# Retention and two MLPs on one core: whole weight rows summed in SBUF, and two changes to when loads are requested

## The chip, the cores and the metric

One core of a Trainium2 chip runs the whole program in one launch. The metric is the device time of one execution in microseconds (us); before is given as the median of three runs, and lower is better. The traces come from the hardware profiler, one execution each.

## The reference

Batch 4, 768 positions, 8 heads of 64, so 3072 tokens of width 512, all in float32. Retention comes first, then a squared-relu MLP (512 to 2048 to 512), then an RMS-normed gated MLP (512 to 1536 to 512):

```python
for t in range(S):
    state = gamma[None, :, None, None] * state + np.einsum('bhd,bhe->bhde', k[:, :, t], v[:, :, t])
    y[:, :, t] = scale * np.einsum('bhd,bhde->bhe', q[:, :, t], state)

h = np.maximum(x @ w_in, 0.0)            # first MLP
x = h * h @ w_out

rms = np.sqrt(np.mean(x * x, axis=-1, keepdims=True) + 1e-06)
xn = x / rms * rms_g                     # second MLP
g = xn @ w_gate
silu = g * (1.0 / (1.0 + np.exp(-g)))
val = xn @ w_val
return (silu * val @ w_out)
```

The weights arrive as 64-bit floats; the kernel turns them into 32-bit ones itself.

## The kernel before

**Products.** Each float32 operand is kept as a high and a low part (`split`: ScalarE casts the high part, VectorE subtracts for the low part), and every product is three matmuls, high by high, high by low, low by high (`mm3`, lines 259 to 261; `proj`, line 301). From the second half of the first MLP on, blocks of 2x2 tiles are multiplied in seven products instead of eight, named P1 to P7. That needs sums and differences of weight tiles ("units"), made once and stored in DRAM: `ui` and `uo` for the first MLP's in- and out-weights, `wu` for the second MLP's gate and value weights, `uo2` for its out-weights. A ring of seven buffers streams them back.

**Stages.** (1) Retention of the first four chunks and the first MLP's block 0 (`block1(0, ...)`, 16 iterations `f`), during which the first MLP's 32 weight tiles are loaded and converted; they stay in SBUF as `W["i", f]` and `W["o", f]`. (2) `block1(1, ...)`, again 16 iterations: per iteration one projection (12 matmuls into `ph`), and the out-products of the iteration before (`out1`, 12 matmuls into `pa` and `pb`); on every even `f` one chunk of retention is visited (`visit`: values, the state, and the next chunk's scores into both `ph` banks). (3) `in_phase` and `in_pair`, then `Out.run`, for the second pair of token blocks, then the third. (4) The second MLP, `pair` by `pair`: six pairs for a block of tokens, each with products P2, P1, P5, P6, P7, P3, P4 (12 matmuls each), then its out-products.

**Order.** The program is scheduled by hand (`tc.manual_schedule`): each engine works in program order. SyncE (SP) issues nearly all DMAs, in program order too, waiting where a buffer or datum isn't ready. `later` collects stores that are issued at the next call of `stores()`. Most tiles come from one pool of 38 slots (`slot`, 128 partitions x 1024 floats). 32 of them are the first MLP's weights in stage 2.

**Making units.** `made_units` takes two tiles `rows` (four weight tiles, whole rows) and makes a sum and differences in five steps, each ended by `yield`: a sum and a difference; the unit P5; P7; P6; P3. P1, P2 and P4 are stored straight from the weights (`keep_units`, `keep_out`, `keep_in`). `whole_rows` fills `rows` for group `q`: for groups 0 and 1 (`2 * q < NCL`) as high + low of the tiles in SBUF, four VectorE sums in two steps; for groups 2 and 3 by two loads from `kept`, to which `finish1` had stored the converted weights in stage 1 (a step of its own, line 1243). In stage 2 `made` (out-weights, groups 0 to 3) is advanced once per even and three times per odd iteration, `made_in` (in-weights, groups 2, 3, 0, 1) once per iteration from `f` = 4 on, and the rest in stage 3.

`tick` converts one weight tile per call (a ScalarE operation, two VectorE ones, and for the second MLP's out-weights a split). After `more_steps(W2_SOON)` at `f == MORE_AT` (line 1330) 25 tiles of the second MLP follow, one per iteration, in stage 2's last iterations, stage 3, and the first steps of `Out.run` (`extra1`).

In stage 4's first block of tokens, `pair` also makes the units of gate and value weights (`make_unit`, quarters `q` reloaded from `wq`), and `made_late` (line 173) those of the out-weights: `first`, `second` and `third` are called after P1, after P6 and after P3 of each pair, and advance it once, twice and once. `first` of pair 0 then runs two steps of the last norm (`background`): a `fold` of squares on VectorE and a request for column sums, which TensorE does in `second` (`sums`, line 337), right behind P6.

**Chunks.** After a visit of chunk `c`, `after_visit` requests chunk `c + 2`: `load` (v and k in natural order, line 892 or 894), then `load_q` (line 902), then `load_k` (line 907). GpSimd scales v (`decay_v`, line 935) and q (`decay_q`, line 924) in later iterations.

Of the kernel before, what the change touches and what calls it, by code (L numbers as in the profile page):

```python
# [38 lines left out]
COMING = (0, 1, 2, 5, 8, 9, 13, 16, 17, 18, 19, 20)  # L39
AHEAD = 5  # L40
EARLY = 24
MORE_AT = 9
W2_SOON = 25
X_AT = (11, 12, 17, 18, 23, 24)

# [13 lines left out]
def retention_then_two_mlps(  # L59
# [16 lines left out]
    uo2 = [[dram.tile([128, 2, 512], F32, name=f"up{q}{k}") for k in range(7)] for q in range(NQ2)]  # L76
    wu = [[dram.tile([128, 2, 512], F32, name=f"wu{n}{k}") for k in range(7)] for n in range(NPR)]
    rows2 = [[dram.tile([128, 2, 512], F32, name=f"rows_p{q}{r}") for r in range(2)] for q in range(NQ2)]
    kept = {(k, n): dram.tile([128, 2, 512], F32, name=f"rows_{k}{n}") for k in "io" for n in range(NCL, 2 * NQ)}

    ones = const.tile([128, D], F32, name="ones")
    g_sb = const.tile([128, KC], F32, name="g_sb")
# [4 lines left out]
    def slot(name, dt=F32):  # L87
        return wp.tile([128, 2, 512], dt, tag="w", name=name)
# [39 lines left out]
    def finish1(key, f, eng=None):  # L128
        t = slot(f"w_{key[0]}{key[1]}", F32R)
        W[key] = t  # L130
        nc.scalar.copy(t[:, 0, :], f)  # L131
        if key[1] >= 2 * NCL:
            nc.sync.dma_start(kept[key[0], key[1] // 2][:, key[1] % 2, :], f)
        return lambda: low(eng or nc.vector, t[:, 1, :], f, t[:, 0, :])

    row_tiles = {}
# [34 lines left out]
        yield  # L171

    def made_late():
        for q in range(NQ2):
            rows = [slot("rows") for _ in range(2)]
            for to, kept_rows in zip(rows, rows2[q]):
                nc.sync.dma_start(to, kept_rows)
            yield
            yield from made_units(uo2, q, rows, lambda: slot("sm")[:, 0, :])

    def finish2(key, f):
        k, n = key
# [26 lines left out]
    def magnitude(i):  # L209
        if i < upto[0] and i not in sizes:  # L210
            key = steps[i][1]
            if key[0] == "p":
                sizes[i] = row_of(key[1])
            elif key[0] in "io" and key[1] >= 2 * NCL and i % 3 == 0:
                sizes[i] = tp.tile([128, TB], F32, tag="y", name="f")
            else:
                sizes[i] = cf.tile([128, 512], F32, tag="f", name="f")
            nc.scalar.activation(sizes[i], loads[i].bitcast(F32)[:, :, 1], AF.Prelu, scale=REBIAS, alpha=NEGATIVE)
# [646 lines left out]
    with tc.manual_schedule():  # L865
# [17 lines left out]
        def load(c):  # L883
            if c < NCH:
                both[c] = rp.tile([128, 2, 512], F32, tag="vk", name="vkt")
                chunk[c] = [None, None] + [both[c][:, i].rearrange("p (a h d) -> p a h d", a=NP, h=2) for i in range(2)]
                if c > CB:
                    load_v(c)

        def load_v(c):  # L890
            if c // B == CPB - 1:
                nc.sync.dma_start(both[c][:, 0], vk[c][:, 0])
            else:
                nc.sync.dma_start(both[c], vk[c])
# [142 lines left out]
        def after_visit(c, x, kv):  # L1037
            x.put(columns_of(c), halves())
            take_state(c, kv)
            load(c + 2)  # L1040
            load_q(c + 2)
            load_k(c + 2)

        decays = slot("decays")
        given, factors = (xp.tile([6 * NP, C + 2 * 512 + H], dt, tag="x", name="factors") for dt in (F32, F32R))
# [112 lines left out]
        def first_states(f):  # L1158

            if f == 2:  # L1160
                take_state(0, into_state(0))
            if f == 0:
                decay_q(CB, nc.vector)
            if f == 1:
                load(CB + 1)
                load_q(CB + 1)
                decay_v(CB, nc.gpsimd)
                decay_v(1, nc.gpsimd)
            for c, n in ((1, 2), (2, 5), (3, 9)):
                if f == n - 1:  # L1170
                    load_kn(c)
                if f == n and c > 1:
                    decay_v(c, nc.vector)
            if f == 2:
                decay_q(CB + 1, nc.vector)
            if f == 3:
                nc.sync.dma_start(g_sb, rmsg)
# [60 lines left out]

        def whole_rows(key, q):
            rows = row_tiles[key, q] = [slot("rows") for _ in range(2)]  # L1240
            if 2 * q >= NCL:
                for r in range(2):
                    nc.sync.dma_start(rows[r], kept[key, 2 * q + r])
                yield
                return
            for r in range(2):
                for c in range(2):
                    w = W[(key, 4 * q + 2 * r + c)].bitcast(F32)
                    plus(rows[r][:, c, :], w[:, 0, :], w[:, 1, :])
                yield  # L1250
# [74 lines left out]
        def last1(f):  # L1325
            stores()
            if f >= RING_AT:
                more_ring()
            next(made, None)
            if f == MORE_AT:  # L1330
                more_steps(W2_SOON)
            if f > MORE_AT:
                tick()
            if f >= 4:
                next(made_in, None)
            if f in (10, 12, 14):
                next(coming_xs)
# [95 lines left out]
        coming_x = raw_x(xs2, X)  # L1433

        def extra1(n, y):
            if n < 3:
                stores()
                tick()
            if n == NOUT - 8:
# [142 lines left out]
        for s in range(NS):  # L1582
# [5 lines left out]
            for p in range(NPR):  # L1588
# [8 lines left out]
                        next(making, None)  # L1597

                def first():
                    make_late(1)  # L1600
                    if p == 0:
                        background()
                        background()
# [4 lines left out]

                def second():
                    nonlocal coming  # L1610
                    make_late(2)
                    if p == 0 and due:
                        sums(pb[1])
                    background()
# [122 lines left out]
```

## Time and profile before

| | |
|---|---|
| median of three runs | 1104.53 us (1103.72 to 1105.84) |
| the profiled execution | 1104.13 us |
| its span, first to last instruction | 1102.4 us |
| TensorE busy | 1083.9 us, 98% of the span |
| VectorE / ScalarE / GpSimd busy | 793.6 / 573.5 / 77.1 us |
| mean granted clock of TensorE | 0.994 |
| DMA | 299.82 MB, 272 GB/s over the span |

Idle time of VectorE or ScalarE counts only where TensorE ends up waiting for it. A trace row gives the start and the duration in us, engine, line, operation, out<-in by the names of the tiles, shape, and count; in brackets stands the idle time of that engine before it and what ended it. Matmuls are pipelined, so the time between two starts says more than a duration: 12 matmuls of 512 columns take about 2.72 us from start to start.

### The profile page before, as it was taken

How to read it: one execution, taken by the hardware profiler on the slowest of the kernel's cores; microseconds unless marked ns; L12 is line 12 of the kernel's file. 1: busy time of each engine (PE TensorE's matmuls, PEld its weight loads, DVE VectorE, ACT ScalarE, POOL GpSimd, SP SyncE). 2: the span in 40 equal slices, each digit the busy share in tenths (PEclk: the TensorE clock that was granted, in tenths of full speed). 3: DMA queues.
4: the chain of work that ended last, by engine and by line, in shares of the span. 5: the costliest groups of instructions: out<-in, count | busy, mean ns of one | idle time of the engine just before them, and what ended most of it. 6: DMA issues, size and time to landing. Idle time of an engine off the chain costs nothing.

```text
span 1102.4 us, 16685 instructions
## 1 busy us (share of the span) xinstructions
PE 1083.9 (98%) x6281; PEld 890.5 (81%) x6281; DVE 793.6 (72%) x1103; ACT 573.5 (52%) x880; POOL 77.1 (7%) x65
## 2 busy tenths in 40 slices
PE   9999999899999999999999989999999999999998
PEld 7888888678878888888888768788888888888887
DVE  6988687699948995678778877996333797333585
ACT  5776445567666546784456545553232554333442
POOL 3000142214320000000000000000000000000000
PEclk9999999899999999999999989999999999999999
DMA  9869699999999679976558989767667567656663
GB/s 363 310 226 324 237 318 362 365 374 352 355 407 317 214 256 382 377 269 208 201 189 309 367 302 343 251 211 252 197 210 270 193 210 249 195 194 196 196 211 116
DMA packets 108164, 299.82 MB, mean 272 GB/s; under 512 B 11012, under 2 KB 34332, under 8 KB 108084
## 3 DMA queue, kind: packets, MB, share of 16 engines
q1 hardware_dynamic: 107904, 298.51, 76.8%
q8 instruction: 50, 0.82, 0.3%
q10 hardware_dynamic: 180, 0.24, 0.1%
q14 instruction: 30, 0.25, 0.1%
HBM read 210.09 MB, written 88.62 MB: 271 GB/s over the span
## 4 chain that ended last, share of the span: by engine, by line
PE 82%; DMA 7%; DVE 6%; ACT 2%; issue 1%; SPq 1%; POOL 0%; DVEq 0%; POOLq 0%; ACTq 0%
PE ph L301 9%; PE ph L259 9%; PE ph L260 9%; PE ph L261 9%; PE pa L259 7%; PE pa L261 7%; PE pa L260 7%; PE pb L259 4%; PE pb L261 4%; PE pb L260 4%; PE pr L259 3%; PE pr L261 3%; PE pr L260 3%; DMA rows<-rows_p 1%; DMA ui<-made 1%
## 5 line engine op out<-in xcount | busy, mean ns | idle before, releaser
L482 ACT CAST o<-act 128x1024 fp32r<-128x1024 f32 x101 | 105.6, 1052 | 111.2 <-DVE act L107 53.5
L100 DVE TENSOR_TENSOR o<-act,o 128x1024 fp32r<-128x1024 f32 x101 | 122.9, 1219 | 27.9 <-ACT o L482 27.8
L260 PE MATMUL ph<-o,ring 128*128 128x512 f32 x228 | 88.6, 389 | 0.0
L259 PE MATMUL ph<-o,ring 128*128 128x512 f32 x228 | 88.5, 388 | 0.0
L261 PE MATMUL ph<-o,ring 128*128 128x512 f32 x228 | 88.5, 388 | 0.0
L259 PE MATMUL pb<-xop,ring 128*128 128x512 f32 x192 | 76.3, 397 | 5.2 <-DVE part L110 4.0
L301 PE MATMUL ph<-xh,w_i 128*128 128x512 f32 x248 | 81.1, 390 | 0.0
L259 PE MATMUL ph<-xop,ring 128*128 128x512 f32 x192 | 75.3, 392 | 1.1 <-DVE part L110 0.6
L261 PE MATMUL pb<-xop,ring 128*128 128x512 f32 x192 | 75.7, 394 | 0.0
L260 PE MATMUL pb<-xop,ring 128*128 128x512 f32 x192 | 75.7, 394 | 0.0
L259 PE MATMUL pa<-xop,ring 128*128 128x512 f32 x192 | 74.9, 390 | 0.0
L260 PE MATMUL ph<-xop,ring 128*128 128x512 f32 x192 | 74.8, 389 | 0.0
L261 PE MATMUL ph<-xop,ring 128*128 128x512 f32 x192 | 74.7, 389 | 0.0
L261 PE MATMUL pa<-xop,ring 128*128 128x512 f32 x192 | 74.7, 389 | 0.0
L260 PE MATMUL pa<-xop,ring 128*128 128x512 f32 x192 | 74.7, 389 | 0.0
L107 DVE TENSOR_TENSOR act<-act 128x1024 f32<-128x1024 f32 x60 | 73.1, 1219 | 0.3
L110 DVE TENSOR_TENSOR part<-pr,part 128x512 f32<-128x512 f32 x38 | 25.8, 689 | 54.4 <-ACT part L114 53.1
L114 ACT COPY part<-ph 128x512 f32<-128x512 f32 x52 | 30.3, 589 | 57.8 <-PE ph L261 57.8
L760 ACT ACTIVATE t<-part 128x512 f32<-128x512 f32 x54 | 34.1, 632 | 49.8 <-DVE part L110 49.8
L301 PEld LDWEIGHTS ph<-xh,w_i 128*128 128x128 f32 x248 | 46.5, 188 | 10.3 <-ACT w_o L131 0.4
L260 PEld LDWEIGHTS ph<-o,ring 128*128 128x128 f32 x228 | 42.8, 188 | 9.3 <-DVE o L100 0.4
L259 PEld LDWEIGHTS ph<-o,ring 128*128 128x128 f32 x228 | 42.8, 188 | 8.9
(255 smaller groups left out, 2632.3 us busy)
## 6 DMA issues: line engine op xcount, KB each, us to landing
ring<-wu SPq DMA_DIRECT2D x84, 512.0 KB, 4.3
ring<-up SPq DMA_DIRECT2D x63, 512.0 KB, 4.2
ring<-uo SPq DMA_DIRECT2D x56, 512.0 KB, 4.3
ring<-ui SPq DMA_DIRECT2D x42, 512.0 KB, 7.2
wu<-ring SPq DMA_DIRECT2D x42, 512.0 KB, 6.0
raw<-w1i SPq DMA_DIRECT2D x16, 512.0 KB, 7.4
raw<-w1o SPq DMA_DIRECT2D x16, 512.0 KB, 8.4
vkt<-vk SPq DMA_DIRECT2D x16, 512.0 KB, 5.1
```

Of the source, the lines that this page charges most:

```text
L100: eng.tensor_tensor(out=dst_l, in0=src, in1=dst_h.bitcast(F32), op=ALU.subtract)
L107: eng.tensor_tensor(out=out_, in0=a, in1=b, op=ALU.subtract)
L110: eng.tensor_tensor(out=out_, in0=a, in1=b, op=ALU.add)
L114: nc.scalar.copy(dst[:, m], acc[m])
L259: nc.tensor.matmul(acc, ah, bh, start=start, stop=False, **more)
L260: nc.tensor.matmul(acc, ah, bl, start=False, stop=False, **more)
L261: nc.tensor.matmul(acc, al, bh, start=False, stop=stop, **more)
L301: nc.tensor.matmul(h, w[:, a, k * 128:(k + 1) * 128], x[b][k], start=n == 0, stop=n == len(order) - 1)
L482: nc.scalar.copy(h, src)
L760: nc.scalar.activation(t, g, AF.Silu)
```

## The change

Five edits. `finish1` no longer stores converted weights to DRAM, `kept` goes, and `whole_rows` makes every group as sums of the tiles in SBUF (so its tiles `f` all come from one pool). `made_in` starts at iteration 1 instead of 4 and is advanced twice in iterations 5 to 8; `MORE_AT` goes from 9 to 12, and `extra1` does six conversions instead of three. `made_late` requests the rows of group `q + 1` in the fourth step of group `q`, and is advanced two, one and one times in pairs 0 to 2, then once each. `load_v` is called after `load_q` and `load_k` in `after_visit`.

```diff
-MORE_AT = 9
+MORE_AT = 12
...
     def finish1(key, f, eng=None):
...
-        if key[1] >= 2 * NCL:
-            nc.sync.dma_start(kept[key[0], key[1] // 2][:, key[1] % 2, :], f)
...
     def made_late():
+        def fetch(q):
+            rows = [slot("rows") for _ in range(2)]
+            for to, src in zip(rows, rows2[q]):
+                nc.sync.dma_start(to, src)
+            return rows
+
+        rows = fetch(0)
         for q in range(NQ2):
-            rows = [slot("rows") for _ in range(2)]
-            for to, kept_rows in zip(rows, rows2[q]):
-                nc.sync.dma_start(to, kept_rows)
             yield
-            yield from made_units(uo2, q, rows, lambda: slot("sm")[:, 0, :])
+            for n, _ in enumerate(made_units(uo2, q, rows, lambda: slot("sm")[:, 0, :])):
+                if n == 3 and q + 1 < NQ2:
+                    coming = fetch(q + 1)
+                yield
+            if q + 1 < NQ2:
+                rows = coming
...
-            elif key[0] in "io" and key[1] >= 2 * NCL and i % 3 == 0:
-                sizes[i] = tp.tile([128, TB], F32, tag="y", name="f")
...
-                if c > CB:
-                    load_v(c)
-
         def load_v(c):
+            if c >= NCH:
+                return
...
             load(c + 2)
             load_q(c + 2)
             load_k(c + 2)
+            load_v(c + 2)
...
                 load(CB + 1)
+                load_v(CB + 1)
                 load_q(CB + 1)
...
         def whole_rows(key, q):
             rows = row_tiles[key, q] = [slot("rows") for _ in range(2)]
-            if 2 * q >= NCL:
-                for r in range(2):
-                    nc.sync.dma_start(rows[r], kept[key, 2 * q + r])
-                yield
-                return
             for r in range(2):
                 for c in range(2):
                     w = W[(key, 4 * q + 2 * r + c)].bitcast(F32)
                     plus(rows[r][:, c, :], w[:, 0, :], w[:, 1, :])
                 yield
...
-            if f >= 4:
+            if f:
+                next(made_in, None)
+            if 4 < f < 9:
                 next(made_in, None)
...
-            if n < 3:
+            if n < 6:
                 stores()
                 tick()
...
                 def first():
-                    make_late(1)
+                    make_late(2 if p < 3 else 1)
...
                 def second():
                     nonlocal coming
-                    make_late(2)
+                    make_late(1)
```

## Rows read from the trace of the kernel before

**Rows 1.** What TensorE waited for: total us, times, longest.
```profile
PE pb L259 <- DVE part L110: 4.0, 1, 4.0
PE ph L947 <- issue: 4.7, 1, 4.7
...
PE pa L260 <- DVE s L100: 0.7, 1, 0.7
PE pa L947 <- POOL qnt L924: 0.7, 1, 0.7
PE ph L259 <- DVE part L110: 0.6, 1, 0.6
```

**Rows 2.** Stretches: length, busy us per engine, granted clock, DMA share, GB/s.
```profile
188.91:202.77 13.86, 13.86 (x129) 11.44 (x128) 6.34 (x13) 7.69 (x13) 3.40 (x3) 1.00 1.02 377
202.77:224.49 21.72, 17.02 (x130) 13.71 (x129) 18.28 (x31) 11.95 (x21) 4.09 (x3) 0.84 0.97 356
573.05:592.93 19.88, 19.88 (x101) 16.06 (x100) 14.22 (x23) 9.96 (x17) 0.00 (x0) 1.00 0.90 326
...
633.02:659.51 26.49, 22.08 (x85) 17.38 (x84) 19.31 (x33) 10.16 (x19) 0.00 (x0) 0.87 0.85 317
659.51:678.67 19.16, 19.16 (x85) 15.85 (x84) 12.67 (x21) 9.92 (x19) 0.00 (x0) 1.00 0.81 296
```

**Rows 3.** VectorE in order of time, near 200 us.
```profile
205.88 0.69 DVE L110 TENSOR_TENSOR sm<-rows 128x512 f32<-128x512 f32 x1 [7.62 <-DMA rows<-rows_o]
```

**Rows 4.** ScalarE in order of time, near 200 us.
```profile
206.61 0.62 ACT L103 CAST made<-sm 128x512 fp32r<-128x512 f32 x1 [7.25 <-DVE sm L110]
```

**Rows 5.** VectorE in order of time, near 650 us.
```profile
650.25 0.69 DVE L110 TENSOR_TENSOR sm<-rows 128x512 f32<-128x512 f32 x1 [3.37 <-DMA rows<-rows_p]
...
653.49 1.28 DVE L110 TENSOR_TENSOR part<-pb,part 128x512 f32<-128x512 f32 x2
```

**Rows 6.** Two sums of high and low parts on VectorE.
```profile
145.88 1.28 DVE L110 TENSOR_TENSOR rows<-w_o 128x512 f32<-128x512 f32 x2
```

**Rows 7.** Stretches 124 to 150, 150 to 175 and 175 to 198, together.
```profile
sum 74.00, PE 74.00 PEld 60.93 DVE 60.00 ACT 37.51 POOL 27.22; mean PE 24.67 PEld 20.31 DVE 20.00 ACT 12.50 POOL 9.07
```

**Rows 8.** The stretch of the first half of one mask.
```profile
121.96:122.93 0.97, 0.97 (x5) 0.79 (x6) 0.91 (x4) 0.12 (x1) 0.00 (x0) 1.00 0.59 220
```

**Rows 9.** VectorE and GpSimd in order of time, near 154 us.
```profile
154.40 1.67 DVE L110 TENSOR_TENSOR sm<-rows 128x512 f32<-128x512 f32 x1
...
153.78 1.73 POOL L378 TENSOR_TENSOR y<-y 128x512 f32<-128x512 f32 x1
```

**Rows 10.** The page's 40 slices, tenths: VectorE busy, TensorE's granted clock.
```profile
DVE  6988687699948995678778877996333797333585
...
PEclk9999999899999999999999989999999999999999
```

**Rows 11.** SP's issues in order of time, near 307 us.
```profile
306.60 0.33 SPq L892 DMA_DIRECT2D vkt<-vk  x1
307.83 0.39 SPq L902 DMA_DIRECT2D qnt<-qT  x1
```

**Rows 12.** SP's issues of the second MLP's rows, groups 0 and 2.
```profile
577.30 1.63 SPq L177 DMA_DIRECT2D rows<-rows_p  x2
...
641.54 1.94 SPq L177 DMA_DIRECT2D rows<-rows_p  x2
```

**Rows 13.** The chain of waits, 573 to 600 us: start, us, what.
```profile
577.80 6.82 DMA rows<-rows_p
```

**Rows 14.** VectorE in order of time, near 580 us.
```profile
579.92 1.94 DVE L110 TENSOR_TENSOR sq<-sq 128x1024 f32<-128x1024 f32 x2
...
585.99 0.69 DVE L110 TENSOR_TENSOR sm<-rows 128x512 f32<-128x512 f32 x1
```

**Rows 15.** TensorE in order of time, near 584 us.
```profile
584.02 0.64 PE L337 MATMUL pb<-sq,ones 128*32 128x128 f32 x16
```

**Rows 16.** ScalarE in order of time, near 139 us.
```profile
138.73 0.62 ACT L103 CAST made<-rows 128x512 fp32r<-128x512 f32 x1 [2.98 <-PE pb L261]
```

More of the change, by code (lines that the diff above doesn't have):

```diff
@@ L78, in retention_then_two_mlps @@
     rows2 = [[dram.tile([128, 2, 512], F32, name=f"rows_p{q}{r}") for r in range(2)] for q in range(NQ2)]
-    kept = {(k, n): dram.tile([128, 2, 512], F32, name=f"rows_{k}{n}") for k in "io" for n in range(NCL, 2 * NQ)}
     ones = const.tile([128, D], F32, name="ones")
```

## The prediction, made before the result was known

> **What bounds the kernel now.** I read the page first: TensorE is busy 98% of the span, so nothing but its few idle microseconds, and the stretches in which its clock is low, can be won. The list of what TensorE waited for [rows 1] names those idles; the five that the change can touch are shown. Two matter: 4.7 us before a chunk's scores and 4.0 us before a product of the second MLP's first block. The table by stretch [rows 2] gives their full price. From one chunk's visit to the next takes 13.86 us, but the stretch from 202.77 takes 21.72, so 7.86 are lost: 4.70 idle, and 17.02 us of TensorE work where 13.86 is normal, that is 3.16 us at the lower of its two levels (1.2 instead of 2.4 GHz; granted clock 0.84). In the first block of the second MLP a quiet pair of steps (from 659.51) takes 19.16 us; the pair from 633.02 takes 26.49, 7.33 lost, of which 22.08 - 19.16 = 2.92 at the low clock.
>
> Next, who was late. At 198 VectorE stands 7.62 us before the first sum over `rows`, until a load of whole rows of the first MLP's out-weights lands [rows 3]. ScalarE, in order, is held 7.25 us at the cast of that sum [rows 4]; the relu that would free the score bank is queued behind it, and TensorE behind that. Before 650.25 it is the same with the second MLP's out-rows: 3.37 us on the load, everything behind it is late, and so is the sum `part` for which TensorE waits [rows 5].
>
> **The change, part by part.**
> 1. *Sums in SBUF for the rows of groups 2 and 3 of both first-MLP matrices.* The load at 195 to 206 is gone, and so is what it holds. The whole 7.86 us of that stretch goes [rows 2], and with it the backlog that makes VectorE late for `s` once more at 239, 0.7 us [rows 1]. I book 7.86 + 0.73 = 8.59.
>
> What it adds: 16 sums of 128x512 (4 groups of 4), two of which take 1.28 us clean [rows 6], so 16 x 0.6 = 9.6 us of VectorE. They come before the time they are needed, since the in-rows now start in iteration 1 instead of 4 and run double-paced in iterations 5 to 8, while the second MLP's conversions start three iterations later. Counting steps iteration by iteration (a sum step 1.2, the five others 1.3, 0.6, 1.2, 1.2, 0.6 us), iterations 1 to 9 get 10.9 us more. Between 124 and 198 VectorE is busy 60.0 of 74 us [rows 7], so 14.0 us are free. It fits, but 3 us from full, and the order within an iteration matters: the first half of a mask, 0.97 us [rows 8], is due within one set of out-products after the scores, 2.7 us (12 matmuls, as in a seventh of the quiet pair). Bounds: 0 (all fits) to 5.8 (one idle of 2.8, as explained under the second rival, plus 3.0 at the low clock). I take 1.0, near the lower end, because TensorE had no idle at all in those 74 us (busy 74.00, the same row) though VectorE worked 81% of them.
>
> GpSimd works for 27.2 us of those 74 [rows 7], and next to it a VectorE sum took 1.67 us instead of 0.64 [rows 6, 9]. The Trainium skill, "SBUF — State Buffer", section "Who interferes with whom", speaks against the change here: a VectorE instruction with two SBUF inputs and a GpSimd one that reads SBUF exclude each other, and the second waits for the first to end; the trace agrees; by that rule, an estimate, each of the 16 sums that meets GpSimd takes 1 us longer, 6 us in all. By rows alone, 16 x (1.67 - 0.64) x 27.2/74 = 6.0, so 16.9 against the 14.0 free, 2.9 us over and inside my bounds; it is one way into the second rival below.
>
> The 16 stores (256 KB) and 8 loads (512 KB) that go are 8.4 of the page's 299.8 MB. TensorE waits for no DMA there other than the ones counted, so nothing more is booked.
>
> 2. *Conversion steps moved.* Three go from iterations 10 to 12 to the out-products' steps 3 to 5, about 1.1 us of VectorE each, into a stretch (the 13th and 14th of the page's slices, 331 to 386) that the page gives VectorE at 8 and 9 tenths [rows 10]. TensorE was not idle there, and operands are prepared three products (8 us) ahead. Bounds 0 to 3.3; I take 0.
>
> 3. *A chunk's q, k ahead of its v.* At 316 TensorE waits 0.73 us for GpSimd's scaling of q [rows 1]. That q was requested at 307.83, 1.23 us after the v [rows 11]. Moved to the front, it is requested 1.2 us earlier and no longer shares the engines with that v: the wait goes, -0.73. The v, now last of the three, is due one visit later; 0. Bounds -0.73 to 0.
>
> 4. *Out-rows of the second MLP one group ahead.* For groups 1 and 2 the load is now issued some 15 to 20 us ahead. Pair from 633.02: the 3.37 us wait goes and one low part (0.6) moves to the next slot of work, so `part` starts at 653.49 - 3.37 - 0.6 = 649.5 and ends at 650.8; TensorE's previous product ends about 650.0. An idle of 0.75 us is left of 4.0, and I book no low clock behind it: the page's row of granted clocks is below 9 tenths, apart from the last slice, in two only, those of the two long idles [rows 10]. With the 0.4 us of other idle in the pair (26.49 - 22.08 - 4.00) that stays, the pair takes about 20.5 instead of 26.49: -6.0. In the pair before it, the second slot of work loses 1.2 us of VectorE, and the 0.6 us idle of rows 1 goes: -0.6. The earlier fetch of group 1 puts 1 MB before some reloads of quarters; at 326 GB/s [rows 2] up to 3.2 us later; I take 0, since VectorE's pause below lets the queue drain.
>
> But group 0 cannot be fetched ahead: the first call issues its load, and *the same slot of work now makes the second call*, whose first instruction sums the rows just asked for. Before, that call stood half a pair later. Its place is the pair from 573.05. SP issues that load at 577.30 [rows 12]. It lands between 584.62, where the chain of waits has its second half landing [rows 13], and 585.99, where VectorE ran that sum without a gap [rows 14]; the load of group 2 took from 641.54 to 650.25, 8.7 us [rows 5, 12], which gives 586.0. I take 585.99. VectorE is free at 579.92, where it began the fold of squares [rows 14], and now stands for 6 us. Queued behind: that fold, for the last norm, a gate product, three low parts. TensorE needs the fold first: its column sums, right behind the P6 product, ran at 584.02 [rows 15]. Now: sum and difference from 585.99, 0.69 each, then the fold, 1.94 us [rows 14], so 589.3; the column sums start there instead of at 584.02, 5.3 us idle. Both longer idles of this trace, 4.7 and 4.0, were followed by the low clock at 3.16 and 2.92 us [rows 2]; so +3.0. Together +8.3 (bounds 4.0 without a low clock, to 5.3 + 3.2). By the time VectorE's `part` is due again it has caught up, as the P7 product runs slowly.
>
> **The sum.** -8.59 - 0.73 - 6.0 - 0.6 + 8.3 + 1.0 = -6.6 us. Against the profiled execution's 1104.13 us (span 1102.4, and 1.7 around it, unchanged) that is **1097.5 us**. The profiled execution lies 0.4 under the median 1104.53 of the runs, within their 1103.72 to 1105.84, so I leave it uncorrected.
>
> **Rivals.**
> *The new wait in the first pair costs nothing* (the rows have landed by 580, or the fold is not behind them). Against it: the gapless start at 585.99 shows only that they had landed by then, but the same load took 8.7 us later, and VectorE is in program order throughout that pair. Then 1097.5 - 8.3 = 1089.2. Chance 0.10.
>
> *VectorE becomes the bound of the first MLP's second block once*: the sums collide with GpSimd, or one of them waits for a buffer. For it: at 138.73 ScalarE waited 2.98 us for the end of a set of out-products before it could write `made` [rows 16], so all 38 slots were taken in iteration 2, and the change asks for two more from iteration 1 on. If VectorE's sum is what waits, the mask stands behind it: two sums and half a mask after the out-products' end, 1.28 + 0.97 and gaps, up to 2.8 us of TensorE (an estimate). Against: the slot may go to the sum at once and the wait to a cast, which has slack. With the low clock 5.8 instead of 1.0: 1102.3; without, 1099.3. Chance 0.16; the dearer case lies about at the edge of what counts as no change, so 0.09 of it is faster and 0.07 within.
>
> *Slower than before, by the same slots in several iterations*: if sums wait at the out-products' end in iterations 1, 2 and 3, that is 3 x 2.8 and 3.0 at the low clock, 11.4 instead of 1.0: 1107.9. It decides from the second such wait on, as all else gains 7.6. For it: an iteration frees two slots and uses one, so the shortage would end only after iteration 3. Against: ScalarE waited only once in before, and a stalled sum delays its own successors' demand. Chance 0.12.
>
> My forecast keeps 0.62, its own range 1094 to 1100.5. **Chances:** 0.2% (about 2.2 us) is what a measurement of this kernel can tell from no change. Faster: 0.62 + 0.10 + 0.09 = 0.81; within: 0.07; slower: 0.12. **Range:** 1089 (the first rival) to 1103 (the second), leaving out the third and some of the edges.
>
> **What would show it.** Right: no idle before the scores near 202, about 13.9 us from visit to visit throughout; no load of rows in the first MLP; the pair from about 640 at 20 to 21 us; a new idle of about 5 us before the column sums over `sq`, released by VectorE's fold, with the low clock behind it, and VectorE's wait for `rows` in front. Wrong: column sums on time (then about 1089); an idle before a first-MLP projection near 120 to 150 that ends with a mask (second or third rival); idles over 1 us in the pairs behind the first (the earlier fetch delays quarters).

## The result, and the profile of the changed kernel

The changed kernel takes **1110.98 us** (median of 6, 1109.77 to 1113.30) against 1103.84 (6 runs, 1102.71 to 1105.84) for the kernel before: a ratio of 1.0063, 95% interval 1.0050 to 1.0077. It is slower by 7 us where 6.6 us less was forecast. Its profiled execution took 1111.17 us with a span of 1109.5, 7.1 more than before. Lines of the helpers have moved up by one (109 is the sum, 106 the difference, 99 the low part, 102 the cast) and the matmuls of the products are on 263 to 265.

What TensorE waited for in the kernel after, which answers to [rows 1] (total us, times, longest):

```profile
PE pb L341 <- DVE sq L109: 5.3, 1, 5.3
PE ph L263 <- ACT part L113: 4.8, 3, 2.8
PE ph L950 <- issue: 4.6, 3, 3.4
PE pb L263 <- ACT part L113: 2.0, 2, 1.5
```

The 4.7 before a chunk's scores and the 4.0 before a product of the second MLP are gone. In their place stand 5.3 before the column sums, 2.8 and 1.5 in the third pair, 1.5 in the sixth, and 3.4 and 0.8 before other scores. The stretches of the kernel after, as in [rows 2] (length; busy us of PE, PEld, DVE, ACT, POOL with instructions; granted clock, DMA share, GB/s). The first seven run from one chunk's visit to the next, the next is all that lies between the two MLPs' stretches, then come the first, third and fourth pair of the second MLP, and its first block's six pairs together:

```profile
119.21:133.08 13.87, 13.87 (x130) 11.45 (x129) 10.74 (x19) 7.20 (x13) 3.63 (x3) 1.00 0.66 216
133.08:146.94 13.86, 13.86 (x129) 11.44 (x128) 10.02 (x15) 5.70 (x11) 5.79 (x4) 1.00 0.76 260
146.94:162.46 15.52, 14.41 (x130) 11.39 (x129) 13.79 (x21) 6.54 (x12) 6.16 (x5) 1.00 0.77 272
162.46:181.44 18.98, 15.63 (x129) 12.73 (x128) 17.78 (x28) 7.57 (x14) 5.39 (x4) 0.91 0.79 272
181.44:195.83 14.39, 14.39 (x137) 11.69 (x136) 13.59 (x24) 7.63 (x14) 4.08 (x3) 1.00 0.85 311
195.83:210.03 14.20, 14.11 (x129) 11.47 (x128) 13.33 (x22) 7.76 (x14) 4.62 (x3) 1.00 0.96 334
210.03:223.89 13.86, 13.86 (x129) 11.45 (x128) 13.64 (x23) 6.96 (x12) 3.76 (x3) 1.00 0.80 261
223.89:572.43 348.54, 347.67 (x2066) 285.93 (x2065) 280.41 (x368) 221.34 (x307) 29.97 (x23) 1.00 0.85 305
572.43:600.32 27.89, 22.61 (x101) 17.92 (x100) 15.50 (x25) 9.95 (x17) 0.00 (x0) 0.88 0.67 245
...
620.18:645.60 25.42, 21.14 (x85) 16.70 (x84) 21.88 (x34) 11.74 (x22) 0.00 (x0) 0.93 0.77 283
645.60:664.75 19.15, 19.15 (x86) 15.69 (x84) 14.86 (x26) 9.84 (x18) 0.00 (x0) 1.00 1.00 374
...
572.43:705.89 133.46, 121.23 (x521) 97.29 (x520) 97.56 (x154) 67.20 (x120) 0.00 (x0) 0.96 0.83 306
```

These add up to the whole difference. The same marks in the kernel before, from its table by stretch:

| stretch | before, us | after, us | difference |
|---|---|---|---|
| start to the first of these visits | 119.05 | 119.21 | +0.16 |
| seven visits of the first MLP's second block | 105.44 | 104.68 | -0.76 |
| from there to the second MLP | 348.56 | 348.54 | 0.0 |
| six pairs of its first block | 125.76 | 133.46 | +7.70 |
| the rest | 403.59 | 403.61 | 0.0 |

The first MLP hides two large numbers behind its small one. The stretch that took 21.72 before (iteration 12's) now takes 13.86, 7.86 less; the visits of iterations 4, 6 and 10 lose 1.66, 5.11 and 0.34, together 7.11 more. In the second MLP the pairs, in order, went from 19.88 to 27.89, 19.34 to 19.86, 20.75 to 25.42, 26.49 to 19.15, 19.16 to 19.86 and 20.14 to 21.28.

**The visit of iteration 6.** VectorE in order of time (start, us, line, operation), then GpSimd, ScalarE and TensorE at the same time:

```profile
157.70 1.78 DVE L99 TENSOR_TENSOR made<-sm,made 128x512 fp32r<-128x512 f32 x1
159.40 1.53 DVE L109 TENSOR_TENSOR sm<-rows 128x512 f32<-128x512 f32 x1
160.96 1.66 DVE L106 TENSOR_TENSOR rows<-rows 128x512 f32<-128x512 f32 x1
162.54 1.76 DVE L99 TENSOR_TENSOR made<-sm,made 128x512 fp32r<-128x512 f32 x1
164.23 0.68 DVE L99 TENSOR_TENSOR s<-r,s 128x512 fp32r<-128x512 f32 x1
...
157.19 1.74 POOL L382 TENSOR_TENSOR y<-y 128x512 f32<-128x512 f32 x1
158.88 1.50 POOL L938 TENSOR_TENSOR vkt<-vkt,vdec_sb 128x512 f32<-128x512 f32 x1
160.34 1.74 POOL L927 TENSOR_TENSOR qnt<-qnt,qdec_sb 128x512 f32<-128x512 f32 x1
162.03 1.73 POOL L382 TENSOR_TENSOR y<-y 128x512 f32<-128x512 f32 x1
...
166.75 0.62 ACT L102 CAST made<-sm 128x512 fp32r<-128x512 f32 x1 [2.90 <-DVE sm L106]
167.28 0.59 ACT L318 ACTIVATE r<-ph 128x512 f32<-128x512 f32 x1
...
167.97 1.56 PE L950 MATMUL ph<-qnt,kTt 64*64 64x128 f32 x32 [3.35 <-issue]
```

Four VectorE instructions that lie beside GpSimd's four take 1.5 to 1.8 us each; the next, with GpSimd done, takes 0.68. VectorE is some 4 us late, ScalarE's cast waits 2.90 for it, the relu behind that cast is what empties the score bank, and TensorE stands 3.35 us until 0.7 after the relu's start. (The releaser is shown as "issue"; in the run without GpSimd's scaling, below, the trace names this relu, `r`, at the same place.) It is the chain of [rows 3, 4], with VectorE's load in the place of the DMA.

**The first pair of the second MLP.** VectorE, then TensorE:

```profile
585.41 0.69 DVE L109 TENSOR_TENSOR sm<-rows 128x512 f32<-128x512 f32 x1 [6.03 <-DMA rows<-rows_p]
586.14 0.69 DVE L106 TENSOR_TENSOR rows<-rows 128x512 f32<-128x512 f32 x1
586.75 1.95 DVE L109 TENSOR_TENSOR sq<-sq 128x1024 f32<-128x1024 f32 x2
...
588.75 1.08 PE L341 MATMUL pb<-sq,ones 128*32 128x128 f32 x16 [5.28 <-DVE sq L109]
```

This is the wait as it was forecast, against [rows 14, 15]: VectorE in front of `rows`, the fold behind it, the column sums 5.28 us late.

**The third pair.** SP's issues in the second pair and, last, VectorE's next step in order of time:

```profile
605.75 0.79 SPq L726 DMA_DIRECT2D q<-wq  x1
...
607.10 1.59 SPq L174 DMA_DIRECT2D rows<-rows_p  x2
608.79 0.94 SPq L726 DMA_DIRECT2D q<-wq  x1
...
611.61 0.46 SPq L726 DMA_DIRECT2D q<-wq  x1
...
621.21 0.69 DVE L109 TENSOR_TENSOR mix<-q,q 128x512 f32<-128x512 f32 x1 [5.58 <-DMA q<-wq]
```

The chain of waits has, between the last two of them (start, us, what):

```profile
611.61 9.57 DMA q<-wq
```

Group 1's rows are now requested in front of the pair's last two quarters. The last quarter takes 9.57 us, and VectorE stands 5.58 before the first step of the next pair's weights. In the kernel before, with those rows behind the last quarter, that quarter takes 5.34 us (chain of waits), and VectorE stands 1.50:

```profile
603.79 5.34 DMA q<-wq
...
609.22 0.69 DVE L110 TENSOR_TENSOR mix<-q,q 128x512 f32<-128x512 f32 x1 [1.50 <-DMA q<-wq]
```

In the changed kernel all that follows on VectorE and ScalarE is late, and TensorE is idle for 1.47 at 629.97 and 2.81 at 635.79, then slow (granted clock of the pair 0.93).

### The profile page after: what moved, and what is told of

Its sections match the earlier page's. It is cut to its first block, busy times and chain, and to the rows that moved or that the text cites. A ratio compares the mean times of both kernels' runs of the same rounds, so it can differ in the third digit from the quotient of the medians.

```text
span 1109.5 us, 16645 instructions
## 1 busy us (share of the span) xinstructions
PE 1085.5 (98%) x6281; PEld 890.7 (80%) x6281; DVE 806.2 (73%) x1119; ACT 571.8 (52%) x880; POOL 76.4 (7%) x65
## 4 chain that ended last, share of the span: by engine, by line
PE 84%; DVE 7%; DMA 4%; ACT 2%; issue 2%; SPq 1%; DVEq 0%; ACTq 0%
PE ph L305 11%; PE ph L263 9%; PE ph L264 9%; PE ph L265 9%; PE pa L263 7%; PE pa L265 7%; PE pa L264 7%; PE pb L263 4%; PE pb L265 4%; PE pb L264 4%; PE pr L263 3%; PE pr L265 3%; PE pr L264 3%; DMA q<-wq 2%; PE pr L996 2%
## 5 line engine op out<-in xcount | busy, mean ns | idle before, releaser
L263 PE MATMUL ph<-xop,ring 128*128 128x512 f32 x192 | 77.2, 402 | 4.8 <-ACT part L113 4.8
L263 PE MATMUL pb<-xop,ring 128*128 128x512 f32 x192 | 75.2, 392 | 2.1 <-ACT part L113 2.0
L264 PE MATMUL ph<-xop,ring 128*128 128x512 f32 x192 | 76.2, 397 | 0.0
L265 PE MATMUL ph<-xop,ring 128*128 128x512 f32 x192 | 75.9, 395 | 0.0
L264 PE MATMUL pb<-xop,ring 128*128 128x512 f32 x192 | 74.8, 389 | 0.0
L265 PE MATMUL pb<-xop,ring 128*128 128x512 f32 x192 | 74.7, 389 | 0.0
L305 PEld LDWEIGHTS ph<-xh,w_i 128*128 128x128 f32 x248 | 46.5, 188 | 10.9 <-DVE causal L973 0.9
```

Source lines behind the costliest of these rows:

```text
L263: nc.tensor.matmul(acc, ah, bh, start=start, stop=False, **more)
L264: nc.tensor.matmul(acc, ah, bl, start=False, stop=False, **more)
L265: nc.tensor.matmul(acc, al, bh, start=False, stop=stop, **more)
L305: nc.tensor.matmul(h, w[:, a, k * 128:(k + 1) * 128], x[b][k], start=n == 0, stop=n == len(order) - 1)
```

## The experiments

Each ratio is to runs of the kernel before on the same chip, with its 95% interval.

### Which half of the change costs what

Part 4 alone in the kernel before:

```diff
+        rows = fetch(0)                # made_late as in the change
...
-                    make_late(1)       # first()
+                    make_late(2 if p < 3 else 1)
...
-                    make_late(2)       # second()
+                    make_late(1)
```

> The kernel before with part 4 of the change alone (out-rows of the second MLP one group ahead, two calls in the first slot of the first three pairs, one in the second). Theory (the loss sits in the second MLP's first block): the seven stretches between its pairs cost 133.5 instead of 125.8 us as in the changed kernel, so 1103.8 + 7.7 = 1111.5 us, with the first MLP as before (4.7 us idle near 206). Rival (the second MLP's loss is an aftermath of the changes in the first MLP, say of the steps that were moved): about 1103.8.

Measured: 1111.99 us, ratio 1.0067 (1.0051 to 1.0084). Its first three pairs take 27.83, 19.80 and 25.09, as in the changed kernel.

The changed kernel with part 4 undone (`made_late` and the calls of the kernel before):

```diff
-                    make_late(2 if p < 3 else 1)
+                    make_late(1)       # first()
...
-                    make_late(1)
+                    make_late(2)       # second()
```

> The changed kernel with part 4 undone. Theory: 1111.0 - 7.7 = 1103.3 us; the first MLP still gains the 7.86 near 202 and loses about as much between 147 and 182 (idles of 0.8 and 3.4 us and the low clock behind them). Rival (aftermath of the first MLP): the second MLP's first block stays at 133.5 and the time at 1111.

Measured: 1102.75 us, ratio 0.9987 (0.9978 to 0.9997), with idles of 0.81 and 3.31 at 150.92 and 168.96, as in the changed kernel. So the two halves add up: against the kernel before they measure +7.9 and -1.4 us, 6.5 together, and the whole change 7.1. Part 4 costs what the changed kernel loses.

### The two losses inside part 4

The calls back to 1, 2, 1 in each pair, the loads still one group ahead:

```diff
-                    make_late(2 if p < 3 else 1)
+                    make_late(1)       # first()
...
-                    make_late(1)
+                    make_late(2)       # second()
```

> The changed kernel with the old number of calls in each slot of work (1, 2, 1), the loads still one group ahead. Theory (two separate losses): the column sums are on time, the first pair 27.9 to 19.9, so 1111.0 - 8.0 = 1103.0 us; group 1 is still requested in front of the last two quarters of its pair, so VectorE still waits some 5.6 us for a quarter and the pair behind it still takes 25.4. Rival (the second loss is the backlog of the first): both go, 1111.0 - 8.0 - 6.3 = 1096.7.

Measured: 1103.83 us, ratio 0.9996 (0.9987 to 1.0005). The first pair is back at 19.88, VectorE's wait for the quarter is still 5.15, and the pair behind it still slow (26.74). Its table by stretch, third pair:

```profile
612.41:639.15 26.74, 22.44 (x85) 17.72 (x84) 22.51 (x35) 11.83 (x22) 0.00 (x0) 0.87 0.81 300
```

The other loss alone, by requesting group 1 behind the quarters:

```diff
         for q in range(NQ2):
+            if q == 1:
+                rows = fetch(1)
             yield
...
-                if n == 3 and q + 1 < NQ2:
+                if n == 3 and q == 1:
...
-            if q + 1 < NQ2:
+            if q == 1:
                 rows = coming
```

> The changed kernel, but group 1 of the out-rows is requested two calls later, in the second slot of the pair, behind the quarters, and summed in the third. Theory (the request ahead of the quarters is what costs the pair from 620): VectorE's wait for the quarter 5.6 to about 1.5 us, that pair 25.4 to about 20, some of it given back as a wait for the rows (0.6 us before the change): about 1106. Rival (not the load, but the two calls in the first slot make VectorE late): the pair stays at 25.4, 1111.

Measured: 1107.46 us, ratio 1.0033 (1.0020 to 1.0047). The third pair in its table by stretch, and VectorE's wait in front of it:

```profile
620.14:639.93 19.79, 19.35 (x85) 15.69 (x84) 18.04 (x29) 10.69 (x20) 0.00 (x0) 1.00 0.91 336
```

```profile
617.03 0.69 DVE L109 TENSOR_TENSOR mix<-q,q 128x512 f32<-128x512 f32 x1 [1.44 <-DMA q<-wq]
```

The request's place alone takes the pair from 25.42 to 19.79, though only 3.5 of these 5.6 us reach the end: 1.4 us above the expected time, with other waits of VectorE for quarters later (1.78 at 658.86). Together the two runs show that the first pair's 8 us belong to the doubled call and the third pair's 5.6 to the place of 1 MB in SP's queue; neither follows from the other.

### What eats the first MLP's gain

The in-rows' steps once per iteration from 2 on:

```diff
-            if f:
-                next(made_in, None)
-            if 4 < f < 9:
+            if f > 1:
                 next(made_in, None)
```

> The changed kernel, but the in-rows' steps run once in each iteration of the first MLP's second block from iteration 2 on (14 steps), not from 1 on and twice in 5 to 8 (19 steps). Theory (two causes: a full set of slots around iterations 2 to 4 costs the visit from 146.9 its 1.7 us; the doubled steps beside GpSimd's work cost the next three visits 6.1 us): the idle of 3.35 before the scores near 168 and the low clock behind it go, 1111.0 - 6.1 = 1104.9 us, and up to 1.7 more where the later start eases the slots. Rival (slots alone): the idle near 168 stays in whole or in part: 1109 to 1111.

Measured: 1109.12 us, ratio 1.0046 (1.0028 to 1.0063). The seven visits take 98.42 instead of 104.68, 6.26 less, and the idles near 150 and 168 are gone. But only 2 us reach the end, 4 less than expected: the five steps that the block no longer does ahead are now due between 218 and 569 (351.04 instead of 348.54), where a new idle of 1.79 stands before a chunk's values at 299.49; 1.2 more lies in front of the block and behind 569, and was not followed.

GpSimd's scaling of q and v left out of that block (its chunks are then not decayed):

```diff
-                    decay_v(at_chunk + 1, nc.gpsimd if j else nc.vector)
+                    j or decay_v(at_chunk + 1, nc.vector)
                     if j:
-                        decay_q(at_chunk + 2, nc.gpsimd)
                         at_chunk += 1
```

> The changed kernel without GpSimd's scaling of q and v in the first MLP's second block (left out, so its chunks are not decayed: GpSimd keeps only the scaling of the states and the sums of squares). Theory (VectorE's sums and differences took 1.5 to 1.8 us instead of 0.6 to 0.7 beside GpSimd, and that is why the relu before the scores near 168 is late): most of those instructions run in 0.7 us, the 3.35 idle goes, 1111.0 - 6.1 = 1104.9. Rival (the doubled steps are too many even when clean, or the slots hold ScalarE): the idle stays at 2 to 3.4, about 1110 to 1111.

Measured: 1104.81 us, ratio 1.0006 (0.9997 to 1.0015). With the same steps at the same places the seven visits take 99.39, 5.29 less; the visit of iteration 4 is whole again (13.91) and of the 3.35 idle 1.49 is left. The run keeps GpSimd's sums of squares (`y`). Of the four VectorE instructions above, the two beside those are as slow as before, and the two with GpSimd done are not (GpSimd, then VectorE):

```profile
155.63 3.44 POOL L382 TENSOR_TENSOR y<-y 128x512 f32<-128x512 f32 x2
...
156.13 1.78 DVE L99 TENSOR_TENSOR made<-sm,made 128x512 fp32r<-128x512 f32 x1
157.84 1.77 DVE L109 TENSOR_TENSOR sm<-rows 128x512 f32<-128x512 f32 x1
159.65 0.69 DVE L106 TENSOR_TENSOR rows<-rows 128x512 f32<-128x512 f32 x1
160.30 0.69 DVE L99 TENSOR_TENSOR made<-sm,made 128x512 fp32r<-128x512 f32 x1
```

So 5.3 of the 7.1 us that the visits lose need GpSimd's scaling beside the extra steps; 1.75 stay in iteration 6 (15.62), with the two instructions that are still slow in front of them. That the time falls by 6.2 and the visits by 5.3 leaves 0.9 that lies elsewhere and was not followed.

One slot of 38 held until the end of iteration 3:

```diff
+            if f == 3:
+                for t in pads:
+                    nc.gpsimd.tensor_tensor(out=t[:, 0, :PQ], in0=t[:, 0, :PQ], in1=t[:, 0, :PQ], op=ALU.add)
...
+        pads = [slot(f"pad{i}") for i in range(1)]
+        for t in pads:
+            nc.gpsimd.memset(t[:, 0, :PQ], 0.0)
```

> The changed kernel with one of the 38 slots held, unused, from before the first MLP's second block to the end of its iteration 3. Theory (slots are short up to iteration 4, VectorE is the bound only behind that): waits of ScalarE on the out-products' end multiply, the visits up to 162 lose 1 to 6 us more, the stretch from 162 on stays within 1 us: 1112 to 1117. Rival (slots cost nothing, VectorE alone does): 1111, every visit as in the changed kernel.

Measured: 1113.56 us, ratio 1.0090 (1.0068 to 1.0111). Iteration 2's visit loses 4.12 (17.99, an idle of 2.22 before a projection), iteration 4's loses nothing, iteration 6's 3.41 instead of 5.11; the seven together take 105.73, 1.05 more than in the changed kernel. In iteration 2's visit, VectorE, then TensorE:

```profile
140.98 1.29 DVE L109 TENSOR_TENSOR rows<-w_i 128x512 f32<-128x512 f32 x2 [5.81 <-PE pb L265]
...
143.16 0.50 PE L305 MATMUL ph<-xh,w_i 128*128 128x512 f32 x1 [2.22 <-DVE causal L973]
```

Two sums wait for the end of the out-products, the mask stands behind them, and TensorE waits for the mask: the second rival's way by a slot, with 2.22 of idle and 1.91 at the low clock where it had 2.8 and 3.0. So one slot less does cost, at once; in the changed kernel itself iteration 2 loses nothing (13.86), so its slots suffice there. The loss of iteration 4 comes of the start in iteration 1 together with GpSimd (either taken away, in the two runs above, takes it away). In the changed kernel two sums at 142.39, ahead of that visit, take 3.12 us beside GpSimd, and a cast of ScalarE at 143.60 waits 2.98 for a store that frees a slot; which of the two counts was not separated.

### Versions that keep the gain

Sums in SBUF with the in-rows' steps once per iteration from 2 on, and the old scheme of part 4 with its calls spread (of the calls, against the kernel before):

```diff
-                    make_late(2)
+                    make_late(2 if p != 3 else 1)      # second()
...
-                    make_late(1)
+                    make_late(1 if p % 2 == 0 else 0)  # third()
```

> A version of its own: the changed kernel with the in-rows' steps once per iteration from 2 on, and for the second MLP's out-rows the old scheme (each group requested in the call before its first use) with the calls spread so that half a pair lies between the two (1, 2, 1 in even pairs, 1, 2, 0 in odd ones, one call fewer in the fourth). Theory: first MLP 8.6 us better than before, less up to 1.7 for the slots; the pairs from 612 and 633 at 19.5 to 20 instead of 20.75 and 26.49, 7.3 better: 1104.1 - 8.6 - 7.3 + 0 to 1.7 = 1088 to 1090. Rival (the pair that loses its wait for rows loses as much to the quarters, queued behind 1 MB of rows): 1094 to 1095.

Measured: 1099.35 us, ratio 0.9960 (0.9945 to 0.9975): faster than both kernels, 10 us worse than expected. The seven visits keep 7.07 of the 7.86; 3.0 go again between 218 and 569 (an idle of 2.31 at 299.73), and the pairs behind the third have idles of 1.00, 1.47 and 2.10, where VectorE waits 2.64 and 1.70 for quarters again.

Then the calls 1, 2, 1 but none in the third slot of the second pair, group 1 requested behind the quarters, group 2 one group ahead, and the conversion steps back where they were:

```diff
-MORE_AT = 12
+MORE_AT = 9
...
-            if n < 6:
+            if n < 3:
...
-                    make_late(1)
+                    make_late(1 if p != 1 else 0)      # third()
```

> Second version: in-rows once per iteration from 2 on, the second MLP's conversion steps where they stood before the change (from iteration 10 on, three behind the out-products); second MLP's rows: calls 1, 2, 1, none in the third slot of the second pair, group 1 requested in the call before (behind the quarters), group 2 one group ahead. Theory: the 2.3 us idle at 300 of the first version (VectorE behind with conversions that were moved to that stretch) goes, and the calls end by the fifth pair, so its last three pairs cost 60 instead of 64: 1099.4 - 3.0 - 3.5 = about 1093. Rival (the first MLP's second block, with sums and conversions both, is too full for VectorE): idles of 1 to 4 us near 200 to 220, 1096 to 1100.

Measured: 1098.02 us, ratio 0.9946 (0.9929 to 0.9963): the rival, 5 us above the expected time. The idle at 300 is gone, and two of 2.4 stand at 211.88 and 224.88 in its place.

The same with the conversion steps where the change has them:

```diff
-MORE_AT = 9
+MORE_AT = 12
...
-            if n < 3:
+            if n < 6:
```

> The second version, but with the conversion steps moved as the change moves them. Theory: the second MLP gains 3.5 us on the first version, the idle of 2.3 near 300 stays: 1099.4 - 3.5 = about 1096, 3 slower than the second version. Rival (that idle has another cause, say the in-rows' steps of groups 0 and 1 alone): both versions show it and come within 1 us of each other.

Measured: 1098.70 us, ratio 0.9949 (0.9933 to 0.9966), with 2.67 idle at 301.25. The expected 3 us between the two are not there. They come within 1 us, but not for the rival's reason: the three conversion steps cost about the same at either place.

And the second version with the in-rows one iteration earlier:

```diff
-            if f > 1:
+            if f:
                 next(made_in, None)
```

> The second version with the in-rows from iteration 1 on (15 steps). Theory (VectorE beside GpSimd is the bound, not the start): within 1 us of the second version. Rival (the start in iteration 1 takes slots that the block needs): an idle of 0.8 us or more near 150 comes back, 1.5 to 2 us slower.

Measured: 1103.22 us, ratio 0.9994 (0.9983 to 1.0005). The visit of iteration 4 takes 15.51 again, with an idle of 0.81 at 151.07. The rival's idle is back, and the early start is a cause of its own; that it acts by slots this run does not show, and its 1.5 to 2 us fall short. Of the 5.2 us between the two versions that visit has 1.65; waits of 0.86 and 1.88 for GpSimd's scaled q near 306 and 319 are new too, the rest lies in several places, and why they came was not followed.

The other way to lose the wait of [rows 3]: rows of groups 2 and 3 still in DRAM, the out-rows requested two calls ahead (no sums; the calls of part 4 as in the version before this):

```diff
         def whole_rows(key, q):
+            if (key, q) in row_tiles:
+                yield
+                return
...
-            yield from made_units(uo, q, row_tiles.pop(("o", q)), lambda: spare)
+            for n, _ in enumerate(made_units(uo, q, row_tiles.pop(("o", q)), lambda: spare)):
+                if n == 3 and NCL <= 2 * (q + 1) < 2 * NQ:
+                    next(whole_rows("o", q + 1))
+                yield
```

> The kernel before with its whole rows still in DRAM, but those of the first MLP's out-weights of groups 2 and 3 requested two calls ahead of their first sum, and the second MLP's calls as in the second version. Theory (VectorE has no room for the 16 sums, the wait of 7.6 us for the rows near 198 was all that was wrong there): the 7.86 near 202 and the 0.7 near 239 go without a loss between 146 and 220, the second MLP's block gains 3.5: 1104.0 - 8.6 - 3.5 = about 1092, 6 better than the second version with its sums. Rival (a load asked for ahead takes slots or DMA time from others, or the block has other limits behind the wait): 1096 to 1100.

Measured: 1097.84 us, ratio 0.9943 (0.9929 to 0.9957), in the rival's range. VectorE's waits for those rows fall to 1.23 at most, no visit up to 204 loses anything, and yet the stretch from 204 still takes 20.16, since a mask is late. The stretch, and TensorE in order of time:

```profile
204.14:224.30 20.16, 16.82 (x130) 13.29 (x129) 18.71 (x32) 10.92 (x20) 4.86 (x4) 0.83 0.97 375
```

```profile
213.26 0.80 PE L312 MATMUL ph<-xh,w_i 128*128 128x512 f32 x1 [3.34 <-DVE causal L981]
```

Behind the wait stood a second limit, VectorE with the conversions. The same with the conversion steps moved as the change moves them:

```diff
-MORE_AT = 9
+MORE_AT = 12
...
-            if n < 3:
+            if n < 6:
```

> The version with the rows requested ahead, and the second MLP's conversion steps moved as the change moves them (three iterations later). Theory (behind the rows' wait stands VectorE's own load in the stretch from 204, with conversions and in-rows together): the stretch 204 to 224 goes from 20.2 to about 14 us, 1097.8 - 6.3 = 1091.5, and up to 2.7 come back as an idle before a chunk's values near 300, where the moved steps land: 1091.5 to 1094. Rival (the stretch is held by its loads of rows, whatever VectorE has to do): it stays over 18 us, 1096 to 1098.

Measured: **1094.43 us, ratio 0.9910 (0.9892 to 0.9928)**, the fastest. The stretch is whole, and so are all seven (97.59 against 105.44):

```profile
203.56:217.43 13.87, 13.87 (x130) 11.45 (x129) 12.65 (x22) 7.70 (x14) 4.08 (x3) 1.00 0.94 306
```

The time is 0.4 above the expected range, and an idle of 1.67 stands at 297.62, where the moved steps land, as expected. Trying to get rid of that one as well:

```diff
-            if f >= 4:
+            if f > 1:
                 next(made_in, None)
+            if 8 < f < 12:
+                next(made_in, None)
```

> The same, with the in-rows' steps from iteration 2 on and twice in 9 to 11 (17 instead of 12 by the end of the block, their rows of groups 2 and 3 still loaded). Theory (the idle near 300 comes of VectorE having both the moved conversions and the in-rows of groups 0 and 1 to do there): no idle near 300, 1091.5, up to 2.7 better than without it. Rival (what is moved forward is late there instead): idles between 180 and 210 of 1 to 3 us, 1093 to 1097.

Measured: 1096.16 us, ratio 0.9925 (0.9907 to 0.9943). The idle at 300 is gone and 3.49 stands before the scores at 195.41: the rival. The work went from one full stretch into another.

## Why the prediction was wrong, point by point

- **The rows' wait, -7.86: right.** That stretch is 13.86 long. It holds in the last version too, where it comes without sums.
- **The 16 sums, +1.0: the first failing step; it measured +7.1** (1.66, 5.11 and 0.34). The step set 10.9 us of work against 14.0 us free between 124 and 198 [rows 7], and took the sums at their clean price. Neither the free time nor the work is spread evenly. These are the visits of iterations 4 and 6 in the kernel before:

```profile
146.79:160.65 13.86, 13.86 (x129) 11.44 (x128) 10.87 (x15) 5.39 (x10) 7.48 (x5) 1.00 0.89 304
160.65:174.52 13.87, 13.87 (x130) 11.45 (x129) 11.08 (x18) 6.53 (x12) 4.03 (x3) 1.00 0.99 325
```

VectorE had 3.0 and 2.8 us free in them; the change brought 2.9 and, among the doubled steps, 6.7 (13.79 and 17.78 us of work in the table above), while 3.1 and 3.8 stayed free in the two visits in front. And the price was not the clean one: beside GpSimd four instructions of 0.7 took 1.5 to 1.8. The prediction had the rows for that [rows 6, 9] and worked out 16.9 against 14.0, then took 1.0 since TensorE had no idle in those 74 us before the change. That an engine at 81% had hidden everything says nothing of what it hides when a stretch of it is filled. With the in-rows from iteration 2 on and once each, 0.8 of the 7.1 is left in the seven visits (98.42 against 97.58 without the long one's loss). The second rival named the mechanism, VectorE beside GpSimd, but priced it for one visit, 5.8; it struck in two. The Trainium skill, "SBUF — State Buffer", section "Who interferes with whom", says that a VectorE instruction with two SBUF inputs and a GpSimd one that reads SBUF take turns; the trace agrees, with 1.53 to 1.78 us beside GpSimd and 0.69 for the same kind where GpSimd's scaling is left out and its sums of squares are done.
- **The small waits near 239 and 316, -0.73 each: not won.** From 224 to 573 both kernels take 348.5. The 0.73 for `s` and the 0.73 for q are gone from the list of waits, others of 0.46, 0.26 and 0.15 are new, and the rest is TensorE's own time (347.67 instead of 347.10); what makes that longer was not followed.
- **The conversion steps moved, 0 (bounds to 3.3): 0 in the changed kernel, not in general.** Where fewer in-rows are done ahead, the moved steps come with idles of 1.7 to 2.7 near 300; where they are not moved, with 2.4 twice near 220.
- **The first pair, +8.3: right, 8.0**, with the idle 5.28 as forecast (5.3) and the low clock behind it.
- **The pair from 633, -6.0: it was -7.34**, the whole loss; the 0.75 of idle that the step left over and the 0.4 of other idle did not come.
- **The pair in front of it, -0.6: the second failing step; it measured +4.7.** The request of group 1 ahead of quarters was seen and bounded at 3.2, and booked at 0 since VectorE's pause in the first pair would let the queue drain. What counted was SP's order: the last two quarters are issued in the second pair, at 608.79 and 611.61, behind the rows at 607.10, whatever was drained before. The bound too was short. It counted the 1 MB at 326 GB/s, 3.2 us; the last quarter took 4.2 longer, the wait rose from 1.50 to 5.58, and TensorE stood idle for 4.3 us of the pair instead of 1.1 and worked 21.1 instead of 19.7, part of it at the low clock. The last two pairs lost another 1.8 (TensorE waits 0.53 at 676.32 and 1.51 at 697.60, where it had waited 0 and 0.79). VectorE's wait for a quarter there is 3.84, but it was 3.42 before; the cause stays open.
- **The sum.** From -6.6 to +7.1 is 13.7: 6.1 from the sums, 5.3 from that pair, 1.8 from the last two, 1.5 from the small waits, 0.5 from the second pair, less 1.6 from the two pairs that came out better. The third rival's 1107.9 is the nearest time, but by luck: its mechanism (TensorE held in iterations 1, 2 and 3 by sums that wait for slots) did not happen, as the first two visits take 13.87 and 13.86.

## What to carry to other kernels

When a transfer is replaced by work on an engine, count that engine's free time stretch by stretch and at the price that it has beside its neighbours, not as one sum over the stage: 14 us free on the whole were 2.8 in the visit that got 6.7 more. When a load is moved ahead, list what it is now ahead of in its queue, and price that by who waits for it. And when one wait is removed, look up what stands behind it: here the same stretch stayed at 20.2 of 21.7 us until VectorE's other work was taken out of it as well.

## What the runs showed of the hardware

A VectorE instruction with one input was slow beside GpSimd as well. In the version that requests its rows ahead, a shift of 128x512 integers took 1.50 us next to GpSimd's 1.73, 0.84 next to GpSimd's 0.93 (at 230.77), and 0.37 to 0.43 where GpSimd was idle. The Trainium skill, "SBUF — State Buffer", section "Who interferes with whom", has this operation among those that can take turns with GpSimd; the trace agrees. VectorE twice, then GpSimd:

```profile
207.81 0.41 DVE L234 TENSOR_SCALAR rows<-rows 128x512 int32<-128x512 int32 x1
...
218.33 1.50 DVE L234 TENSOR_SCALAR rows<-rows 128x512 int32<-128x512 int32 x1
...
217.82 1.73 POOL L935 TENSOR_TENSOR qnt<-qnt,qdec_sb 128x512 f32<-128x512 f32 x1
```

The length of an idle alone did not tell whether TensorE's clock fell behind it. At the same place in two kernels, 3.35 us (the changed kernel) was followed by scores of 1.56 us for 32 matmuls and a granted clock of 0.91 in the stretch, and 3.31 us (part 4 undone) by scores of 0.90 and a clock of 1.00. In the run with one slot held, 2.22 us of idle came with a clock of 0.91. The stretches with part 4 undone, then with one slot held:

```profile
163.50:180.90 17.40, 14.09 (x130) 11.47 (x129) 16.86 (x27) 7.56 (x14) 5.34 (x4) 1.00 0.84 308
135.17:153.16 17.99, 15.77 (x129) 12.54 (x129) 10.50 (x17) 6.43 (x13) 5.98 (x5) 0.91 0.60 198
```

Against the normal 13.87 of TensorE's work these idles cost 1.8 (15.63 in the changed kernel), 0.2 and 1.9 us on top of their length. The 3.0 that the prediction books behind a long idle was near for the 5.28 of the first pair, where 22.61 instead of 19.88 is 2.7, and 1.1 to 2.8 too high for these.
